# Causal attention scores on one Trainium2 core: half-empty diagonal blocks packed into a shared tile, stores in halves, and a new instruction order

## The chip, the core and the metric

The kernel runs on one core of one Trainium2 chip. The core has five engines with instruction streams of their own: PE (TensorE, matrix products into the PSUM memory), DVE (VectorE), ACT (ScalarE), POOL (GpSimd) and SP (SyncE, which here issues all DMAs). They meet only through semaphores. The metric is the time of one execution on the device in microseconds (us); lower is better. A time is given as the median of several runs.

## The reference

The input x has 2048 tokens of 512 channels in bfloat16. Two paths work on it, and a gate for each token mixes them:

```python
g = sigmoid((x * gate_w).sum(-1, keepdims=True))
a = A_ref(x, wq, wk, wv, wo, beta)      # attention with memory
b = B_ref(x, A_re, A_im, ..., Dskip)    # state-space convolution
return g * a + (1 - g) * b
```

Path A has 32 heads of width 16 and works through 4 segments of 512 tokens. Inside a segment it is causal softmax attention; across segments it reads a matrix memory M and a sum z, which are updated after each segment:

```python
for s in range(4):
    logits = einsum('bhqd,bhkd->bhqk', qs, ks) * scale + mask   # key > query is masked
    a_dot = softmax(logits) @ vs
    a_mem = (phi(qs) @ M) / (phi(qs) @ z + 1e-6)
    outs.append(g * a_mem + (1 - g) * a_dot)
    M, z = M + phi(ks).T @ vs, z + phi(ks).sum(tokens)
a = concat(outs) @ wo
```

Path B builds a convolution kernel of length 2048 for each of 512 channels from complex exponentials and convolves x with it by Fourier transforms.

## The kernel before

**Attention.** The function scores (lines 1021 to 1111) is called for each of 4 segments s and 4 groups hg of 8 heads, 16 groups in all. A group's even heads (gi = 0) and odd heads (gi = 1) lie in four strips of 32 partitions, r = 0 to 3, so that four matmuls, one in each strip, make the scores of four heads beside each other. For the odd heads, project (lines 992 to 1016) makes a second copy ko of the keys, in which the even heads' rows are zero (line 1004); mkT is that mask. Scores have keys on the partitions and queries along the free axis. The 512 keys of a segment are four blocks J of 128. Block J is needed by the queries from 128 J on, 512 - 128 J of them, and the first 128 of those form the diagonal block, which is masked.

For a group the scores fill five tiles of 128 partitions x 2048 columns (four heads x 512 columns, four PSUM banks), listed in kinds (lines 1027 and 1028): A0 has block 0 of the even heads, B0 blocks 1 and 3 of the even ones, C block 2 of both, A1 and B1 blocks 0, and 1 and 3, of the odd ones. For each tile the matmuls run (line 1073), then ACT takes the exponential of all 2048 columns into a buffer pT (line 1082). The diagonal is masked in one of two ways: in the first eight groups (pem, NPM = 8) a matmul of the identity with negm adds -30000 before the exponential (lines 1074 to 1081); in the last eight DVE multiplies the diagonal blocks of pT by mask01 (lines 1094 to 1096). The function pv (lines 1032 to 1048) then multiplies with the values: for each block J, each query block tb from J on and each head, one full matmul of 17 columns (16 values and a one, whose sum is the softmax denominator), 40 for one gi, 80 for a group. norm (lines 1050 to 1058) divides.

seg_tokens (line 931) makes the values vp of a segment; seg_state (line 950) updates the memory with buffers ek and rk; ophase (line 1113) reads it into o2 and transposes the sum.

**State-space path.** ssm_prep, ssm_powers and tables (line 1149) build the tables of exponentials, mostly on DVE in groups of two multiplications and an addition with a scratch tile t2. tail (line 1234) runs over 16 tiles t in each of two halves of the channels, named a and b: constants are loaded (CD, CT), x's transform is made and multiplied with the kernel's (line 1286), transformed back, and gathered in V2 with DMAs. At the end of tail, "fin", "fih" and "fir" are PE's operations of the output projection and the last transform; DVE first scales x (line 1332) and then mixes both paths into a tile ou (line 1337), and a DMA of 256 KB stores four token blocks (line 1340).

**What sets the order.** Every operation is recorded through op (line 161), or through dma and evac, which end there, with the tiles that it reads and writes. A string ORDER (lines 366 to 459) holds the order of all 1864 operations, made beforehand: each entry is the operation's number, an "a" or "v" where it is a copy that can run on ACT or on DVE (evac, lines 224 to 233; 166 entries have an a, 88 a v), and the buffers that it takes. replay (line 235) reads it, and emit (line 264) works out the waits and writes one instruction stream for each engine, in that order. Nothing is reordered when it runs. Because matmuls and copies are issued through helpers, the profile shows all matmuls but transposes at line 698, all DMAs at line 222 and the two kinds of copies at lines 226 (ACT) and 227 (DVE).

Scores always take PSUM banks 0 to 3 together (line 1062); pT has four buffers (NPT, line 354). Pools are laid out in lines 612 to 673.

Of the kernel before, what the change touches and what calls it, by code (L numbers as in the profile page):

```python
# [353 lines left out]
NPT = 4  # L354
# [12 lines left out]
21/0 192/0 193 194 195/0 394/0 196/0 10/4 197 208/1 9/3 0/0 26/3/1 15/0 27v 32/0 57/1 7/0 12/0 23/0 20/0 1237/0 16/0  # L367
11/1 17/0 58/0 14/2 13/5 33/0 41/1 42/2 36/3 37 34/9 60/1 35/12 38 39 40/6 1243/3/0 48/4 43/5 3/0 44 45 47/7 49/8
59v/0 46 51/6 50 1245/2 65v/4 53/13 52/10 64/0 591/0 66 1255/4/1 62/0 63 28/5/0 1253/6 54/9 55/0 56 1/0 1244a 76/4
74/1 75 77v/0 61a 203/7/1/2 86/3 89v/3 78 88/2 1254a 87 253/3/2/0 68/2 90 101v/1 70/1 100/3 98/0 99 69 82/6 29a 181/5  # L370
102 113v/2 110/3 80/1 1256a 112/0 81 206/0/0 111 204a 114 30/6/2 254a 1246a 31v 79 205 18/0 207a 184/3 124/7 1258/1
176/4 103 258/2/1/1 380/0 91 222/0/1 592/0 223 1257 122/0 123 593/0 259 134/2 125v/5 67 182/1 135/2 256/1/1 217/3/0/0
215/0 224 179/0 136 218 177/2 180/0 216a 94/3 146/0 115 1247 260 1000v/0 148/0 243/0/3 244 1271/0/1 147 257a 211/2 219
999v 161v/6 178 998v 126 127 162 185 802/0 245 997v 220 1001v/0 149v/7 1002 209/1 163 1272a 212a 231/0/0 232 158/0 233
1006/1 1005 1003/0 199/3 200 137v/8 1004 213/0 1009/0 214a 25 1007 160/5 1011 1259/2/0 210a 150 226/0/2 227 1260a
381/3 159 1269/0 1261/1 382 225/2 151 228 1270a 1008 138 255 1273 139 92/2 1262a 1263 238/3 239/0/1 240 1015/1 229
1010 1014 230 170v/9 1012/0 234 1016 1013 340/0/2 93 171 1023 241 1018/1 235/0 201/0 202/1 341a 236 383 104/3 1276/1/1
265/0/2 266 105/4 237/0 106 1017 172 267 1274/0 242 246 247 1238/2/0 1239a 1024/0 1277a 269/0/3 270 1275a 271 1019
248/1 261 116/3 1240/2 1278 1025 296/0/0/1 1020 297a 249 1250/1/1 1027/1 1241a 1242 274/0/0 275 268/0 272 276 1251a
386/2/1/2 387a 282/0/1 283 1026 284 250 1021/0 117/2 1028 273 277 1029 299/3/0 1248/1 1022 278/2 1036/1 279 385/0 118  # L380
1266/2/0 1300/0 300a 1249a 1267a 286/0/2 287 337/2/2/0 5/0 24 221/3/0 1264/1 280/1 1035 298 1032 1037 130/7 1252 288
1279/1 310/0/3 311 1265a 301/0/0/0 128/0 262 312 281/1 285 289 290 306/0/2 302 307 1038 338a 1039/0 308 1033/1 1040
291/3 1030/0 292 263/0 446/2/1 293 303 342/1/1/1 1031 1295/3/1 323/0/1 304 1297/0 324 343 344 1268 1296a 447a 1298a
1303/1/0 1034 1301/3 1302v 129 325 401/2 1044/0/0 402v 1045 1047/3 1048 183 450/0 142/5 140/2 141 388 345 315/0/0
154/0 1304a 316 339 1050/2 1051 1052v 1041/1 1042 1061v/0 1057v/0 1059v 1063/1 1065 1049a 1060v 1058v 251/3 1046a
309/2 317 107a/4 327/0/2 328 252a/0 1066/0 294/0 313 1299 314 318 803/3 1043a 1062 1067 1064 319/2 389/1/0 1054/0 329
1075/0 1068 320 108 1071 1072/1 152/3 119a/1 390a 1074 321/0 349/0/3 350 1076 804 1285/1/1 83v/0 1084/0 1083 1073
399/2 351 322/3 84 295a 353/0/0 1077 1286a 1305 1085 95v/2 1086 354 1053 326 1287/0 395/1 330 1288v 400a 331 332/3 355
153 1087/1 396a 71a/6 358/0/1 359 305/0 346 1313/2/0 360 1311/1 4/0 85 333 1312a 1055 1289 1088 72 1314a 1078/1 347
334 1095 1096/0 366/0/2 367 1290/1/1 368 109 352/2 1292/0 1293a 1291a 6/0 1056 1315 2/0 1079 73 1097 1080 1294 120 121  # L390
22 493/3/0/1 370/0/3 371 494a 1081/1 1280/0/0 356 357 361 397/1 495 1089 143v/5 1090/0 1282/3 372 1281a 408/0/0 1082
409 1318/0/1 1091 1098 1069/1 362/4 1283a 1284 1070 363 144 1099/0 410 164/1 805 1319a 398a 365/3 412/0/1 413 335/0
369 373 374 364/1 375/5 96 1308/1/0 414 336a 165/6 376 1093/1 1306/2 1309a 425/0/2 426 1092 1307a 1100 97 411/0 1316/1
415 427 1310 1094 1317a 377 166 443/2/2/0 131v/8 132 429/0/0 430 1320 1328/0 1110/1/0 1111 444a 1107/3 1112v 1108
1101/2 167a/3 173v/9 168 1102 1104/1 1105 431 155a/7 198 1118v/0 156 1120v 169 1117a 1123/1 157 1121v/0 417/0/3 174
1330/0 1125 1119v 418 1126/0 445 1122 1127 1131 1132/0 1133 1124 393/1 1106a 416 496/1/2 1382/1 419 497a 1103a 1109a
1128 475/0/1 476 477 1356/2 133 420 1329/0 1116 1113 424/1 391/1 428 1331/2/0 1135/0 421/0 1355/1 1134 1129/1 175 1114
1115 422 451/3/0/0 432 433 434/1 392 1332a 1334 1343/0 1333 458/0/3 459 460 1130 544/2/0 452 423/0 1341/1 1136 1144/1
1143 435 264 462/0/2 594 545a 463 464 1335/0/1 403/2/1/1 145 1342/0 384/0 1145 467/0/0 348 468 436 1336a 461/1 378/0
404 465 1138/0 1147/1 1146 1337/1 453 466 454 405 1137 1139 1148 1141/0 1338/3/0 1156/1 1140 1344/2/1 469 1354/0 1345a  # L400
1339a 479/0/3 480 474/2 1347 1348/3/0 470 379a 481 471/1 1349a 478 523/0/2 1357/0/2 448/0 1346 1368/0 1340/0 524 1358a
1155 1359 472 482 1360 449 406 483 484/3 1361/3/1 407/0/1 1350/0 473/1 1351/1/1 1157 485 1158 1159/1 1367/1 525 1369/0
486 1362a 1381/1 515/0/3 1142 516 437/1/2/0 455 1352a 1353 438 1408/2 1374/1/0 517 456 501/6/1/1 1363/1 1364/7/0 498/1
502 439 440 1160 608/0/1 1365a 1380/0 1370/2/0 503 527/0/0 528 1149 1375a 522/3 8/0 1371a 1150/0 609a 1387/1/1
541/2/1/0 529 526 1383/0/1 654/5/2/2 542a 549/2/0/0 1152 1395/0 1384a 1388a 441/0 1151 1372 1153/1 530 1373 1376/0
1394/0 1154 500/1 600/4/1 550 1377/1/1 655a 487/3/4/1 442a/0 1434/1 1385 1386 1366 1378a 531 499 551 532/5 1167/5/0
1164/0 1161/1 1162 601a 552 602/0 1393/1 1165 488 1166a 533 1407/1 489 1170/2 1168 1169a 1171 1179a/0 1172a 1389/0
1390/0/0 1163a 490 504 1391a 1181v/0 506/0/1 507 1396/2/2 1178v 1186/0 1185 186/1 543 1180v 1177a 1400/0/0 1397a 1187
1182 187/0 1406/0 1379 612/2 1409/1/0 508 1183/1 1192/0 190/0 510/0/0 1401a 1410a 1184 1191 1188 1193 1398 1399 1173
1195/1 595 1194 534/0 1198/0 511 1447/0 1413/0/1 1392 505/1 553 512 1196 613a 1412 1402/1 1189/1 1403/3/1 556/0/2 557  # L410
1203 554 1411 1197 509/2 513 514 518 1190 1414a 535/0/3/0 1415/0 1404a 558 1416/3/0 560/0/3 561 1433/1 519/0 1417a
1199 520 536 1432/1 1460/2 521 1446/0 1445/0 1200 537 1435/3/1 1439/2/0 1405 1204/0 1436a 538 1201/1 1499/1 657/3/2
1437 1321/0 1205 559/0 562 1202 1209 1448/1/2 1438 573/0/1 574 1418 1459/1 658a 1452/3/1 1449a 1440a 1441/1 1451 563
597/2/0/1 575 564 1450 565/0/0 566 1210/0 546/1 598a 1453a 1442/1/1 491/2 1206 1454/0 1211 1207/1 1443a 1472/0 1176
# [114 lines left out]
def build_graph(nc, es, A_x, A_wq, A_wk, A_wv, A_wo, A_beta, B_A_re, B_A_im, B_B_re, B_B_im,  # L529
# [911 lines left out]
```

## Time and profile before

| what | value |
|---|---|
| time, median of 3 runs | 303.54 us (302.54 to 307.06) |
| profiled execution | 304.81 us; its span 303.0 us |
| mean granted TensorE clock in it | 0.963 |
| ACT exponentials of scores, line 1082 | 80, 152.0 us |
| ACT copies, line 226 | 158, 88.9 us busy |
| DVE copies, line 227 | 53 from PSUM in float32, 34.9 us busy |
| DVE masks, line 1094 | 40, 22.5 us busy |
| PE matmuls, line 698 | 3767, 254.7 us busy |
| DMA | 47.85 MB, mean 158 GB/s |

The profile shows one execution. Busy times are unions, so an instruction that overlaps the one before it on its engine adds less to them than its own duration. A line of a group reads: line, engine, operation, destination and source with their partitions x elements, how many; then busy us and mean ns of one; then the idle time of the engine just before them and what ended it. The chain of work follows the last instruction back to what released it at each step. A matmul's end is modelled and includes the draining of the array, so its duration (some 0.17 us for 17 columns) is much longer than the step from one to the next.

### The profile page before, as it was taken

Reading aid. Unit: us, or ns where it says so; the run is one execution under the profiler, and the core shown is the slowest. Engines: PE = TensorE matmul, PEld = TensorE weight load, DVE = VectorE, ACT = ScalarE, POOL = GpSimd, SP = SyncE. Lnnn points to the kernel's source line nnn. Section 1 sums busy time; section 2 is a strip of 40 time slices with the busy share of each in tenths; the row PEclk is TensorE's granted clock in tenths of the full one; section 3 lists DMA queues with packets and bytes.
Section 4 is the critical chain, followed back from the end, with each engine's and each line's share of the span. In section 5 each row is a group of like instructions: output and inputs, shape, how many; then the busy total and the mean of one; then the engine's idle time right before and its main releaser. Section 6 shows DMA issues by size and latency. Waiting matters only on the chain.

```text
span 303.0 us, 9317 instructions
## 1 busy us (share of the span) xinstructions
PE 260.7 (86%) x3855; PEld 176.8 (58%) x3855; DVE 280.6 (93%) x694; ACT 258.4 (85%) x309; POOL 3.3 (1%) x10
## 2 busy tenths in 40 slices
PE   1569799898879867999999999999999998899990
PEld 1334444555544645766766576766677656679870
DVE  3999989999999898999999989998999999998992
ACT  2799999999999998999899999999999899983000
POOL 2000000000000000000000000000000000000000
PEclk9997978999996999999999999999999999999996
DMA  5998422612231464665666667687756677731333
GB/s 140 269 209 190 95 90 71 177 68 60 63 121 50 120 177 122 180 173 149 191 210 164 206 181 236 206 244 216 211 176 208 200 233 235 217 104 27 105 110 111
DMA packets 55546, 47.85 MB, mean 158 GB/s; under 512 B 22736, under 2 KB 50384, under 8 KB 55504
## 3 DMA queue, kind: packets, MB, share of 16 engines
q1 hardware_dynamic: 55504, 47.26, 54.5%
q8 instruction: 30, 0.49, 0.7%
q14 instruction: 12, 0.10, 0.1%
HBM read 29.02 MB, written 6.29 MB: 117 GB/s over the span
## 4 chain that ended last, share of the span: by engine, by line
PE 31%; DVE 27%; ACT 26%; DMA 5%; issue 5%; SPq 4%; DVEq 0%; ACTq 0%
PE psum L698 30%; ACT sb L1082 11%; ACT sb L226 10%; DMA sb<-sb 4%; SPq L222 4%; DVE sb L1337 4%; DVE sb L227 4%; DVE sb L1332 3%; DVE sb L1286 3%; DVE sb L1094 3%; ACT sb L808 3%; DVE sb L1177 2%; DVE sb L1184 2%; DVE sb L1180 2%; DMA sb<-in_B_log_dt_dram 1%
## 5 line engine op out<-in xcount | busy, mean ns | idle before, releaser
L698 PE MATMUL psum<-sb 128*128 128x17 bf16 (+11 forms) x3767 | 254.7, 233 | 24.0 <-ACT sb L1082 11.7
L698 PEld LDWEIGHTS psum<-sb 128*128 128x128 bf16 (+3 forms) x3767 | 169.9, 99 | 104.3 <-ACT sb L1082 27.3
L1082 ACT ACTIVATE sb<-psum 128x2048 bf16<-128x2048 f32 x80 | 152.0, 1900 | 3.4 <-PE psum L698 2.2
L226 ACT ACTIVATE sb<-psum 128x512 bf16<-128x512 f32 (+2 forms) x158 | 88.9, 618 | 8.6 <-PE psum L698 8.1
L227 DVE CAST sb<-psum 128x512 bf16<-128x512 f32 (+1 forms) x53 | 34.9, 671 | 2.4 <-PE psum L698 2.3
L1177 DVE TENSOR_TENSOR sb<-sb 128x512 bf16<-128x512 bf16 (+3 forms) x52 | 34.2, 659 | 0.0
L1180 DVE TENSOR_TENSOR sb<-sb 128x512 bf16<-128x512 bf16 (+3 forms) x52 | 33.7, 654 | 0.1
L1184 DVE TENSOR_TENSOR sb<-sb 128x512 bf16<-128x512 bf16 (+3 forms) x52 | 33.6, 660 | 0.1
L1286 DVE TENSOR_TENSOR sb<-sb 128x1024 bf16<-128x1024 bf16 x32 | 21.4, 678 | 2.2 <-issue 1.3
L1094 DVE TENSOR_TENSOR sb<-sb 128x1024 bf16<-128x1024 bf16 (+1 forms) x40 | 22.5, 573 | 0.4 <-ACT sb L1082 0.4
L1332 DVE SCALAR_TENSOR_TENSOR sb<-sb 128x256 f32<-128x256 bf16 x32 | 14.3, 475 | 0.0
L1337 DVE SCALAR_TENSOR_TENSOR sb<-psum,sb 128x256 bf16<-128x256 f32 x32 | 13.1, 477 | 1.0 <-PE psum L698 1.0
L1057 DVE TENSOR_TENSOR sb<-psum,sb 128x256 bf16<-128x256 f32 x32 | 13.4, 418 | 0.2
L808 ACT ACTIVATE sb<-sb 128x512 f32<-128x512 f32 x18 | 11.5, 654 | 0.0
L1054 DVE RECIPROCAL sb<-psum 128x16 f32<-128x16 f32 x32 | 8.0, 249 | 0.6 <-PE psum L698 0.6
L1134 DVE TENSOR_TENSOR sb<-psum,sb 128x512 bf16<-128x512 f32 x12 | 8.2, 687 | 0.3
L809 DVE TENSOR_TENSOR sb<-sb 128x256 f32<-128x256 f32 x18 | 7.3, 414 | 0.9 <-ACT sb L808 0.9
L1013 ACT ACTIVATE sb<-sb 128x512 bf16<-128x512 bf16 x12 | 7.6, 637 | 0.0
L810 DVE SCALAR_TENSOR_TENSOR sb<-sb 128x256 f32<-128x256 f32 x18 | 7.4, 417 | 0.0
L962 ACT ACTIVATE sb<-psum 128x512 bf16<-128x512 bf16 x12 | 7.4, 614 | 0.0
L756 PE MATMUL psum<-sb 128*128 128x128 bf16 x24 | 2.7, 279 | 5.0 <-DMA sb<-c_ident 4.6
L959 PE MATMUL psum<-sb 128*128 128x128 bf16 x48 | 4.9, 227 | 2.2 <-ACT sb L226 2.2
(67 smaller groups left out, 102.1 us busy)
## 6 DMA issues: line engine op xcount, KB each, us to landing
sb<-c_DNM SPq DMA_DIRECT2D x32, 320.0 KB, 3.5
sb<-c_DNM SPq DMA_DIRECT2D x32, 192.0 KB, 3.0
sb<-sb SPq DMA_DIRECT2D x84, 64.0 KB, 2.9
sb<-in_A_x_dram SPq DMA_DIRECT2D x9, 512.0 KB, 4.9
scr_Z<-sb SPq DMA_DIRECT2D x16, 256.0 KB, 2.3
sb<-scr_Z SPq DMA_DIRECT2D x32, 128.0 KB, 3.1
sb<-sb SPq DMA_DIRECT2D x32, 128.0 KB
out_dram<-sb SPq DMA_DIRECT2D x8, 256.0 KB, 2.2
```

Of the source, the lines that this page charges most:

```text
L226: fa = lambda e: e.activation(dst(), src(), ACT.Copy)
L227: fd = lambda e: e.tensor_copy(dst(), src())
L698: mm = lambda e, o_, l, r_, st, sp, **kw: e.matmul(o_, lhsT=l, rhs=r_, start=st, stop=sp, skip_group_check=True, **kw)
L808: op("ACT", ("As", 512), lambda e, sq=sq, Z=Z: e.activation(ap(sq, n=512), ap(Z, n=512), ACT.Square), r=[Z], w=[sq], key=PW[h] + PWS * k)
L1082: o = op("ACT", ("Ax", 2048), lambda e, P=P, pT=pT: e.activation(ap(pT, n=2048), ap(P, n=2048), ACT.Exp, scale=0.25), r=[P], w=[pT])
L1094: op("DVE", ("V2", 128 * nb), lambda e, pT=pT, dims=dims: e.tensor_tensor(ap(pT, dims=dims + [[1, 128]]), ap(pT, dims=dims + [[1, 128]]), ...
L1177: op("DVE", ("V2" if n > 1 else "V1", 256 * n), lambda e: e.tensor_tensor(run(tile, ne, dst, 1), run(tile, ne, src, sstep), ap(pw, cl * 51 ...
L1180: op("DVE", ("V2" if n > 1 else "V1", 256 * n), lambda e: e.tensor_tensor(run(t2, n, 0, 1), run(tile, ne, src, sstep), ap(pw, cl * 512 + 2 ...
L1184: op("DVE", ("V2" if n > 1 else "V1", 256 * n), lambda e: e.tensor_tensor(D_(), D_(), ap(t2, n * 128, [[-n * 128, 2], [2 * n, 64], [1, 2 * ...
L1286: op("DVE", ("V2", 1024), lambda e, Y=Y, XAB=XAB, K3=K3: e.tensor_tensor(ap(Y, dims=[[512, 2], [1, 512]]), ap(XAB, dims=[[512, 2], [1, 512 ...
L1332: op("DVE", ("V1", 256), lambda e, xd=xd, b4=b4: e.scalar_tensor_tensor(ap(xd, n=256), ap(xns[b4 // 4], (b4 % 4) * 512 + half * 256, n=256 ...
L1337: op("DVE", ("V1", 256), lambda e, ou=ou, b2=b2, j=j, b4=b4, P=P, xd=xds[j]: e.scalar_tensor_tensor(ap(ou, (2 * b2 + j) * 256, n=256), ap( ...
```

## The change

**Scores.** The queries of a diagonal block's first half need only the block's first 64 keys. These parts, for all four blocks, for even and odd heads and for two neighbouring groups hg and hg + 1, go into one "low" tile: the even heads' 64 keys on partitions 0 to 63, the odd heads' 64 keys on partitions 64 to 127, 64 queries for each block, 4 blocks x 2 groups x 64 = 512 columns for each of 4 strips. The other tiles begin at each block's query 64: A has blocks 0 and 3 (448 + 64 columns), B blocks 1 and 2 (320 + 192). So two groups have nine tiles of 2048 columns, where they had ten, and the tile C is made in even groups only. ko is laid out anew (192 columns for each block: 64 of the even rows, then 128 of the odd), by two DVE instructions, of 512 and 256 elements, in place of one. Both groups of a pair are projected together.

**Masks.** In A and B a mask now covers 64 columns at two places, 128 columns for each strip. The low tile is masked on DVE, 2048 elements in one instruction, in all 16 groups (DQL = 1); its matmul mask is left out.

**Values.** pv leaves out the diagonal block: 24 full matmuls for one gi. A new function pvd makes the diagonal at the end of each gi, with pairs of matmuls on half of the array's columns each: 64 queries from the low tile with vL, 64 from pT with vp, 32 of them for one gi. vL is a copy of the values in which the odd heads' values of each block's first 64 keys stand on partitions 64 to 127: two DMAs of 136 KB for each segment, and one clearing by POOL at the start. The values are now stored with even heads first, then odd.

**Stores and buffers.** Each output store of 256 KB becomes two of 128 KB, each as soon as its half is made. Buffers: pT 4 to 3, plus one for the low tile; ek, o2 and t2 2 to 1; CT of half b 5 to 4; vL has one.

**Order.** ORDER is another one, with 1873 entries; 186 have an a, 68 a v. It is left out below.

```diff
-NPT = 4
+NPT = 3
+NPL = 1
+DQL = 1
...
-        op("DVE", ("V4", 512), lambda e: e.tensor_scalar(ap(ko, n=512), ap(kT, n=512), ap(mkT, n=1), None, ALU.mult), r=[kT, mkT], w=[ko])
+        op("DVE", ("V4", 512), lambda e: e.tensor_scalar(ap(ko, 64, [[192, 4], [1, 128]]), ap(kT, dims=[[128, 4], [1, 128]]), ap(mkT, n=1), None, ALU.mult), r=[kT, mkT], pw=[ko])
+        op("DVE", ("V4", 256), lambda e: e.tensor_scalar(ap(ko, dims=[[192, 4], [1, 64]]), ap(kT, dims=[[128, 4], [1, 64]]), ap(mkT, 1, n=1), None, ALU.mult), r=[kT, mkT], pw=[ko])
...
+        for gi in range(2):
+            S.dma(lambda gi=gi: ap(vL, 272 * gi, [[544, 4], [1, 272]], p0=64 * gi, np_=64), lambda gi=gi: ap(vp, 272 * gi, [[544, 4], [1, 272]], np_=64),
+                  139264, r=vparts + [vp] + ([vL] if s == 0 else []), pw=[vL])
...
-                for tb in range(J, 4):
+                for tb in range(J + 1, 4):
...
+        def pvd(gi):
+            T = PV[gi]
+            src = [q[1:] for q in diag if q[0] == gi]
+
+            def f(e):
+                for J, pT, off in src:
+                    for r in range(4):
+                        o = (4 * hg + r) * 17 + J * 544 + gi * 272
+                        mm(e, ap(T, J * 68 + r * 17, n=17, np_=64), ap(low[0], r * 512 + (hg % 2) * 256 + J * 64, n=64), ap(vL, o, n=17), False, True, tile_position=(0, 0))
+                        i = mm(e, ap(T, J * 68 + r * 17, n=17, p0=64, np_=64), ap(pT, r * 512 + off, n=64), ap(vp, o, n=17), False, True, tile_position=(0, 64))
+                return i
...
+            ent = [] if isl else [(1, 0), (2, 320)] if nm[0] == "B" else [(0, 0), (3, 448)]
...
+                if isl:
+                    for h_, (q_, _, k_, _, _) in enumerate(two):
+                        for J in range(4):
+                            for r in range(4):
+                                i = mm(e, ap(P, r * 512 + 256 * h_ + 64 * J, n=64), ap(k_, 192 * J, n=128, p0=32 * r, np_=32),
+                                       ap(q_, 128 * J, n=64, p0=32 * r, np_=32), h_ == 0 and J == 0, not pem or bool(DQL), tile_position=(32 * r, 0))
+                    return i
...
-            S.dma(lambda g4=g4: bass.AP(out, g4 * 2048 + half * 256, [[8192, 128], [512, 4], [1, 256]]),
-                  lambda ou=ou: ap(ou, dims=[[256, 4], [1, 256]]), 262144, r=[ou])
+                S.dma(lambda g4=g4, b2=b2: bass.AP(out, g4 * 2048 + b2 * 1024 + half * 256, [[8192, 128], [512, 2], [1, 256]]),
+                      lambda ou=ou, b2=b2: ap(ou, b2 * 512, [[256, 2], [1, 256]]), 131072, r=[oup[b2]])
...
-            project(s, hg)
+            if hg % 2 == 0:
+                S.key = TA0 + GA * (i0 - 4)
+                project(s, hg)
+                project(s, hg + 1)
```

316 lines of the change are left out of this document (166 added, 150 removed).

## The prediction

> **What bounds the kernel now.** I read the page first: the busy shares, the forty slices, and the chain that ended last.
>
> ```profile
> span 303.0 us, 9317 instructions
> ...
> PE 260.7 (86%) x3855; PEld 176.8 (58%) x3855; DVE 280.6 (93%) x694; ACT 258.4 (85%) x309; POOL 3.3 (1%) x10
> ...
> PE   1569799898879867999999999999999998899990
> ...
> DVE  3999989999999898999999989998999999998992
> ACT  2799999999999998999899999999999899983000
> ...
> PEclk9997978999996999999999999999999999999996
> ...
> PE 31%; DVE 27%; ACT 26%; DMA 5%; issue 5%; SPq 4%; DVEq 0%; ACTq 0%
> ```
>
> Three engines are full at once. DVE leads with 280.6 us. The chain is shared almost equally (31, 27 and 26%), so it hops between engines that are full, and a saving on one engine alone is paid out only where the chain lies on it. The windows view splits the span into the stretch in which the attention exponentials set the pace, the stretch in which both halves of the state-space path run beside them, and the end.
>
> ```profile
> core 0: us, PE busy (x) PEld busy (x) DVE busy (x) ACT busy (x) POOL busy (x), PEclk, DMA share, GB/s
> 6.00:128.00 122.00, 98.66 (x1444) 58.23 (x1445) 116.76 (x305) 116.75 (x153) 0.65 (x1) 0.93 0.49 130
> 128.00:236.00 108.00, 104.93 (x1653) 74.27 (x1652) 103.68 (x242) 103.43 (x122) 0.66 (x1) 1.00 0.67 199
> 236.00:297.00 61.00, 56.05 (x755) 43.53 (x752) 58.77 (x144) 36.67 (x33) 0.00 (x0) 1.00 0.51 153
> ```
>
> The reader should see that PE has room only in the first stretch (98.66 of 122). In the second all three are at 96 to 97%. In the third DVE leads (58.77 of 61), PE follows, and ACT has nothing to do near the end.
>
> **The change on ACT and DVE.** The durations are in the groups by shape, and in the chain, which shows what each instruction adds when it follows another.
>
> ```profile
> L1082 ACT ACTIVATE sb<-psum 128x2048 bf16<-128x2048 f32 x80 | 152.0, 1900 | 3.4 <-PE psum L698 2.2
> L227 DVE CAST sb<-psum 128x512 bf16<-128x512 f32 x50 | 33.5, 682 | 1.5 <-PE psum L698 1.3
> L1094 DVE TENSOR_TENSOR sb<-sb 128x1024 bf16<-128x1024 bf16 x24 | 16.3, 679 | 0.4 <-ACT sb L1082 0.4
> L1177 DVE TENSOR_TENSOR sb<-sb 128x2048 bf16<-128x2048 bf16 x12 | 14.6, 1215 | 0.0
> L1094 DVE TENSOR_TENSOR sb<-sb 128x512 bf16<-128x512 bf16 x16 | 6.6, 414 | 0.0
> L817 DVE CAST sb<-sb 128x512 bf16<-128x512 f32 x15 | 6.2, 419 | 0.0
> L1004 DVE TENSOR_SCALAR sb<-sb 128x512 bf16<-128x512 bf16 x16 | 5.5, 347 | 0.4 <-ACT sb L226 0.4
> L818 DVE TENSOR_SCALAR sb<-sb 128x256 bf16<-128x256 bf16 x20 | 4.4, 227 | 0.0
> ```
>
> ```profile
> 20.22 2.43 ACT sb L226 x5
> 161.62 1.14 DVE sb L1177
> 185.34 1.78 ACT sb L1082
> 189.61 1.20 DVE sb L227 x2
> 295.40 1.57 DVE sb L1337 x4
> ```
>
> A DVE evacuation of 512 columns lasts 0.68 but adds 0.60 (1.20 for two), so about 0.08 of each DVE instruction lies under its neighbour. An ACT evacuation adds 0.49 (2.43 for five), an exponential 1.78.
>
> Exponentials: 16 groups with 5 tiles are 80; afterwards 16 with 4 and one tile for each of 8 pairs are 72. ACT loses 8 x 1.78 = 14.2 us.
>
> Evacuations moved: in the order's list the entries marked for ACT go from 166 to 186, those marked for DVE from 88 to 68. Twenty move. Laid against the order in which the code makes the operations, 13 of them net are PSUM evacuations of 512 columns; the other seven are four casts of powers (the row of L817), one table copy, one lag-table evacuation and one transposed input, on average 0.4 for DVE and 0.5 for ACT. DVE loses 13 x 0.60 + 7 x 0.4 = 10.6; ACT gains 13 x 0.49 + 7 x 0.5 = 9.9. ACT net: -4.3.
>
> Masks on DVE: before, the last eight groups have 16 of 512 and 24 of 1024 elements, 16 x 0.414 + 24 x 0.679 = 22.9. Afterwards they have 32 of 512, and every pair, those of the first eight groups too, has one of 2048: 32 x 0.414 + 8 x 1.215 = 23.0. The sum is the same, but 4 x 1.14 = 4.6 us of it come into the first groups, which had none on DVE.
>
> The second masked copy of the keys: 16 of 256 elements, 0.227 - 0.08 = 0.15 each, 2.4 us (between 16 x 0.08 and 16 x 0.35, the row of L1004; nearest is L818, the same form and size). DVE net: -10.6 + 0.1 + 2.4 = -8.1 us.
>
> **The change on PE.** Short windows, each cut around one operation, price it; x also counts up to five matmuls of the neighbours that reach in. In order: one scoring tile of 4 matmuls of 512 columns, 32 or 16 rows each, which run beside each other; 16 full matmuls of 17 columns; 4 full ones of 512; 64 of 40 columns on half the array's columns each; a scoring tile of two widths; 4 mask matmuls of 2 x 128; 8 of 128.
>
> ```profile
> 187.17:187.50 0.33, 0.33 (x4) 0.10 (x5) 0.33 (x1) 0.33 (x1) 0.00 (x0) 1.00 0.59 157
> 187.50:187.91 0.41, 0.41 (x20) 0.41 (x17) 0.41 (x2) 0.40 (x2) 0.00 (x0) 1.00 0.10 25
> 188.34:189.21 0.86, 0.86 (x6) 0.39 (x4) 0.86 (x2) 0.86 (x1) 0.00 (x0) 1.00 0.79 279
> 170.68:171.81 1.12, 1.12 (x68) 1.09 (x65) 1.12 (x3) 1.06 (x2) 0.00 (x0) 1.00 0.60 170
> 184.43:184.76 0.33, 0.33 (x9) 0.12 (x9) 0.33 (x2) 0.33 (x2) 0.00 (x0) 1.00 1.00 374
> 162.43:162.87 0.44, 0.44 (x6) 0.38 (x4) 0.44 (x2) 0.44 (x2) 0.00 (x0) 1.00 1.21 233
> 162.87:163.31 0.44, 0.44 (x10) 0.44 (x8) 0.44 (x2) 0.44 (x2) 0.00 (x0) 1.00 0.81 313
> ```
>
> So a full matmul of 17 columns adds 0.0256 us, a half one 0.0175. A change between full array and row strips costs about 0.11 (0.33 for the strips against 0.86 / 4 = 0.22 for the same 512 columns).
>
> Values: a group's 80 full matmuls become 48 full and 64 halves, which come in two blocks of 32. Removed 32 x 0.0256 = 0.82; added 64 x 0.0175 = 1.12, and two entries into the half arrangement at 0.1. That is +0.5 for a group, +8 for 16. Lower end: a pair of halves for one full, and no change of arrangement that was not there, 0. Upper end: every half as a full one, +1.02 for a group, +16. I take +8, from the row that has halves.
>
> Scores: tiles of 448 + 64 and 320 + 192 columns cost 0.33, as both rows of scoring tiles show, whatever the widths. Two C tiles (0.66) become one low tile of 32 small matmuls: at least 0.33 (512 columns again), at most 32 x 0.0256 + 0.11 = 0.93. I take the middle, 0.6: 8 x (0.6 - 0.66) = -0.5 (-2.6 to +2.2).
>
> Masks by matmul, first eight groups only: 2 tiles of 4 x 0.055 and 3 of 4 x 0.11 (1.76) become 4 tiles of 4 x 0.055 (0.88); the low tile has none. -7.0.
>
> PE net: +8 - 0.5 - 7.0 = +0.5 us; but -3.2 for the first eight groups, where PE has room, and +3.8 for the last eight, where it has hardly any.
>
> The Trainium skill, TensorEngine Tiling (Array Packing), Performance Considerations, says that each matmul carries about 60 cycles of overhead, and that one with free dimension 1 takes as long as one with 60. TensorE: Matmul & The Clock Gate, Back-to-back issue gap, gives that floor as about 25 ns. Full matmuls here agree (0.0256); the halves do not (0.0175). By the rule the values would cost PE +16 in place of +8.
>
> **DMA, POOL, buffers.**
>
> ```profile
> sb<-sb SPq DMA_DIRECT2D x84, 64.0 KB, 2.9
> out_dram<-sb SPq DMA_DIRECT2D x8, 256.0 KB, 2.2
> ```
>
> Two copies of 136 KB for each segment shift the values' first 64 keys for the odd heads. The nearest row, copies of 64 KB inside the buffer memory, lands after 2.9; I take 3 for these. The copies' tile has one buffer, so a segment's copies wait for the last value matmuls of the segment before, and behind them on SP stand the loads of the tail's constants. In the new order 4 to 6 us of DVE work (by the durations above) lie between each second copy and its first reader: covered, and 4 x 3 = 12 us if that cover is gone. POOL clears that tile once, beside 300 us of idle POOL: nothing. The stores: the last one starts with its last half only. Between the last DVE instruction (295.40 + 1.57 = 297.0) and the end lie 6.0 us, of which landing is 2.2; half the bytes give at most 1.1, I take -0.4. Its eight more issues lie between DVE instructions of the end: nothing.
>
> Buffers go from two to one for ek, o2 and t2, from five to four for CT of the second half, from four to three plus one for the exponentials. ek and o2 are needed once in a group, t2's readers and writers are all on DVE in order with a multiplication between: nothing, and at most 52 x 0.08 = 4 us for t2. The exponentials' buffers are the rival below: a buffer is now held until the diagonal's value matmuls.
>
> **The sum.** DVE -8.1, ACT -4.3, PE +0.5. By the chain's shares of 303 us: DVE 82 us x 8.1 / 280.6 = -2.4, ACT 79 x 4.3 / 258.4 = -1.3, PE 94 x 0.5 / 260.7 = +0.2, end of store -0.4: -3.9. The profiled execution took 304.81 (span 303.0 and 1.8 around it) and would become 300.9. The median of the three runs is 1.3 below it, and the prediction is a median: 303.5 - 3.9 = 299.6.
>
> **The rivals.**
>
> *DVE is the one bound.* It is busy 279.2 of the 291 us before 297, and the end is its own. Then all of -8.1 and the store's -0.4 come out: 295.0. Against it: PE's 97% in the second stretch.
>
> *PE takes over.* From 128 on, PE has 3.1 + 5.0 us idle, and the last eight groups give it 3.8 more. If it is the bound there, DVE's saving is lost and the time is 303.5 + 3.8 - 0.4 = 306.9. Against it: PE's busy time contains the draining of matmuls, so there is more room than it shows.
>
> *A half matmul costs as much as a full one.* A mechanism of the value blocks alone: +7.6 for the last eight groups in place of +3.8, with PE the bound: 303.5 + 7.6 - 0.4 = 310.7. That is the rule of the Trainium skill above, taken for halves. The 64 halves in 1.12 us speak against it.
>
> *The low tile's chain holds PE.* This is the one on the slower side. PE works in order.
>
> ```profile
> PEld psum L698 <- ACT sb L1082: 27.3, 50, 1.5
> PE psum L698 <- ACT sb L1082: 11.7, 23, 1.4
> PEld psum L698 <- DVE sb L1094: 1.7, 6, 0.6
> ```
>
> PE waits for exponentials already, but hardly for masks. Now the diagonal's value matmuls need the low tile's exponential (1.78), its mask on the fullest engine (1.14) and their own 0.56: 3.5 us from scores to the release of two buffers, of which the fourth exponential needs one. Behind them on PE stand the next scores, and ACT waits for those. Uncovered in all 8 pairs it is 28 us, and 36% of that takes 299.6 past +2%; with half of it the time is 313.6. Against it: the new order puts 8 to 25 other PE operations between a low tile's scores and its first reader.
>
> **How the numbers follow.** A measurement of this kernel tells about 2% (6.1 us) from no change. My forecast, the shared chain, 299.6 with its own range 296.5 to 303: 0.38. DVE alone, 295.0: 0.29. PE takes over, 306.9: 0.15. Halves as full, 310.7: 0.04. The low tile's chain, 313.6: 0.14. Faster by over 2% is below 297.4: the DVE case and a small part of the first, 0.32. Slower by over 2% is above 309.6: the last two, 0.18. Within 2%: 0.50. The range leaves out those last two, 0.18: from 293.2 (DVE alone, with the store's 1.1 and the key copies at 0.08: 295.0 - 0.7 - 1.1) to 308.2 (PE's takeover with the last four low tiles at 0.93: 306.9 + 4 x 0.33).
>
> **What would show it.** ACT: 72 exponentials, about 254 us busy. DVE about 272. PE about 261, with a block of 32 half matmuls in 0.56 and the low tile in 0.33 to 0.93. If PE waits for the mask of 2048 elements, the low tile's chain is right; if PE is above 98% from 128 us on while DVE falls below 92%, PE took over. The prediction is wrong in its core if DVE's busy time falls by 8 and the span by 8 too, or if no engine's sum moves as stated.

## The result, and the profile after

The changed kernel takes 302.62 us (median of 20 runs, 299.32 to 307.61), the kernel before, on the same chip, 304.38 us (20 runs). The ratio is 0.990, with an interval from 0.987 to 0.993. A second measurement of the same kernel, called again below, gave 303.06 against 304.53 us, ratio 0.994 (0.991 to 0.997). The change saves 1.8 to 3.0 us by these two ratios, about 0.6 to 1.0%. The first ratio leaves out the six slowest of the changed kernel's 20 executions and none of the other kernel's; the medians of all of them differ by 1.8 us, a ratio of 0.994 like again's. All lines of the changed kernel are from again, whose profiled execution took 303.31 us; its mean granted clock was 0.936, the median of again's runs is 0.952.

The page of the changed kernel, with the rows that answer to those of before: span, busy time, slices, granted clock, chain.

```profile
span 301.5 us, 10764 instructions
...
PE 257.8 (86%) x4554; PEld 184.1 (61%) x4591; DVE 272.6 (90%) x690; ACT 253.4 (84%) x321; POOL 5.2 (2%) x11
...
PE   2668598978788799889999899989999999999990
...
DVE  1999999889999999899999998699888998887992
ACT  2899999999999999989999999888998999982100
...
PEclk9999576699789879999999999999999999999997
...
ACT 33%; PE 32%; DVE 26%; issue 3%; DMA 3%; SPq 1%; DVEq 0%
```

DVE's busy time fell by 8.0 (280.6 to 272.6), ACT's by 5.0 (258.4 to 253.4), PE's by 2.9 (260.7 to 257.8). The span fell by 1.5. So most of it became idle time: DVE's idle time in the span grew from 22.4 to 28.9, ACT's from 44.6 to 48.1. The same stretches as before, the last one cut at 299 in place of 297:

```profile
core 0: us, PE busy (x) PEld busy (x) DVE busy (x) ACT busy (x) POOL busy (x), PEclk, DMA share, GB/s
6.00:128.00 122.00, 98.90 (x1690) 61.14 (x1706) 117.78 (x310) 116.60 (x163) 0.66 (x1) 0.86 0.52 138
128.00:236.00 108.00, 102.14 (x1940) 76.04 (x1963) 100.59 (x243) 98.66 (x121) 0.66 (x1) 1.00 0.67 195
236.00:299.00 63.00, 55.85 (x921) 46.16 (x914) 54.19 (x139) 36.08 (x37) 0.00 (x0) 0.99 0.55 164
```

In the second stretch all three engines have room now (102, 101 and 99 of 108; they had 105, 104 and 103). No engine is full, and yet the kernel is hardly faster. What fills the room stands in the view of waits, first of the changed kernel, then of the one before, over the whole span:

```profile
ACT sb L226 <- PE psum L705: 15.1, 22, 4.2
PE psum L705 <- ACT sb L1133: 9.4, 14, 2.1
...
DVE sb L227 <- PE psum L705: 4.9, 7, 1.6
ACT sb L1133 <- PE psum L705: 4.7, 12, 0.6
...
DVE sb L1376 <- DMA sb<-in_A_x_dram: 1.7, 1, 1.7
...
PEld psum L705 <- DVE sb L1141: 0.2, 1, 0.2
```

```profile
ACT sb L226 <- PE psum L698: 8.1, 15, 2.2
DVE sb L227 <- PE psum L698: 2.3, 6, 1.0
ACT sb L1082 <- PE psum L698: 2.2, 7, 0.5
```

ACT waits for PE 19.8 us where it waited 10.3, DVE's evacuations (its copies out of PSUM) 4.9 where they waited 2.3. PE in its turn waits 9.4 for exponentials (11.7 before). New is the wait of DVE for a load of x. Part of ACT's wait lies in the last stretch, where ACT has nothing to do anyway; in the second stretch alone (128 to 236 us) the copies of both engines wait longer for PE too, first the changed kernel, then the one before:

```profile
ACT sb L226 <- PE psum L705: 5.7, 13, 1.2
DVE sb L227 <- PE psum L705: 4.9, 7, 1.6
```

```profile
ACT sb L226 <- PE psum L698: 2.5, 8, 0.5
...
DVE sb L227 <- PE psum L698: 1.0, 4, 0.4
```

### The profile page after: what moved, and what is told of

The parts are those of the page before. It is cut to its first block, busy times and chain, and to the rows that moved or that the text cites. A ratio compares the mean times of both kernels' runs of the same rounds, so it can differ in the third digit from the quotient of the medians.

```text
span 305.8 us, 10764 instructions
## 1 busy us (share of the span) xinstructions
PE 256.7 (84%) x4554; PEld 184.5 (60%) x4591; DVE 272.6 (89%) x690; ACT 253.2 (83%) x321; POOL 5.2 (2%) x11
## 4 chain that ended last, share of the span: by engine, by line
ACT 38%; PE 34%; DVE 16%; DMA 5%; issue 3%; SPq 1%; DVEq 0%; ACTq 0%
PE psum L705 34%; ACT sb L1133 19%; ACT sb L226 13%; DMA sb<-sb 4%; ACT sb L815 3%; DVE sb L1227 2%; DVE sb L1381 2%; DVE sb L1329 2%; DVE sb L227 2%; DVE sb L1223 1%; ACT sb L976 1%; DVE sb L1220 1%; ACT sb L823 1%; SPq L222 1%; DMA sb<-c_ident 1%
## 5 line engine op out<-in xcount | busy, mean ns | idle before, releaser
L705 PE MATMUL psum<-sb 128*64 128x17 bf16 (+11 forms) x4466 | 250.2, 222 | 33.1 <-ACT sb L1133 10.7
L705 PEld LDWEIGHTS psum<-sb 128*128 128x128 bf16 (+3 forms) x4503 | 177.9, 104 | 103.4 <-issue 24.2
L1133 ACT ACTIVATE sb<-psum 128x2048 bf16<-128x2048 f32 x72 | 137.6, 1911 | 7.6 <-PE psum L705 7.0
L226 ACT ACTIVATE sb<-psum 128x512 bf16<-128x512 f32 (+2 forms) x173 | 99.4, 636 | 17.6 <-PE psum L705 17.1
L227 DVE CAST sb<-psum 128x512 bf16<-128x512 f32 (+1 forms) x39 | 26.1, 673 | 6.3 <-PE psum L705 6.0
L1141 DVE TENSOR_TENSOR sb<-sb 128x512 bf16<-128x512 bf16 (+1 forms) x40 | 22.6, 570 | 1.9 <-ACT sb L1133 1.9
L763 PE MATMUL psum<-sb 128*128 128x128 bf16 x24 | 3.1, 310 | 6.0 <-DMA sb<-c_ident 5.1
L227 DVE COPY sb<-psum 128x1024 bf16<-128x1024 bf16 x2 | 2.6, 1280 | 6.2 <-PE psum L763 6.2
```

What stands on the lines that cost most here:

```text
L226: fa = lambda e: e.activation(dst(), src(), ACT.Copy)
L227: fd = lambda e: e.tensor_copy(dst(), src())
L705: mm = lambda e, o_, l, r_, st, sp, **kw: e.matmul(o_, lhsT=l, rhs=r_, start=st, stop=sp, skip_group_check=True, **kw)
L1133: o = op("ACT", ("Ax", 4 * W), lambda e, P=P, pT=pT, W=W: e.activation(ap(pT, n=4 * W), ap(P, dims=[[512, 4], [1, W]]), ACT.Exp, scale=0.2 ...
L1141: op("DVE", ("V2", 2048 if isl else 512), lambda e, pT=pT, md=md, m0=m0: e.tensor_tensor(ap(pT, dims=md + [[1, 64]]), ap(pT, dims=md + [[1 ...
```

## The experiments

Ratios are to the kernel before, measured beside each kernel, with their intervals. The theory behind the prediction was that the chain is shared and a saving is paid by the chain's shares. The rivals were one engine as the bound. A number of us got from two ratios carries their intervals, some 1.3 us either way.

**The same kernel again, and one engine relieved at a time.** The reliefs leave work out. For PE, pvd's second half of blocks:

```diff
                 for J, pT, off in src:
+                    if J > 1:
+                        continue
```

For DVE, the masks' width; for ACT, the exponentials' columns from the fifth group on:

```diff
-                    ap(pT, dims=md + [[1, 64]]), ap(pT, dims=md + [[1, 64]]), ap(mask01, m0, [[0, k_[1]] for k_ in md] + [[1, 64]]), ALU.mult),
+                    ap(pT, dims=md + [[1, 16]]), ap(pT, dims=md + [[1, 16]]), ap(mask01, m0, [[0, k_[1]] for k_ in md] + [[1, 16]]), ALU.mult),
...
-            o = op("ACT", ("Ax", 4 * W), lambda e, P=P, pT=pT, W=W: e.activation(ap(pT, n=4 * W), ap(P, dims=[[512, 4], [1, W]]), ACT.Exp, scale=0.25), r=[P], w=[pT])
+            o = op("ACT", ("Ax", 4 * W), lambda e, P=P, pT=pT, W=W: e.activation(ap(pT, dims=[[512, 4], [1, 448 if 4 * s + hg > 3 else 512]]), ap(P, dims=[[512, 4], [1, 448 if 4 * s + hg > 3 else 512]]), ACT.Exp, scale=0.25), r=[P], w=[pT])
```

> The changed kernel once more, timed beside the others. Shared chain (my forecast's theory: three engines take turns, PE is short of room from 128 us on): 0.985 to 0.993 of before, and in an undisturbed profile DVE's idle time grows by what its busy time fell, while ACT and DVE wait longer for PE than before (before: ACT copies for PE 8.1 us, exponentials for PE 2.2 us). Low tile's chain: PE waits for DVE's masks of 2048 elements, over 3 us in all (before 2.1 us for all masks).

> The changed kernel with the diagonal's value matmuls of blocks 2 and 3 left out (16 of 32 halves in each block, so the output is not the reference's): PE loses 512 x 0.0175 = 9.0 us, half of it in the last eight groups, nothing else changes. Shared chain: a third to a half of it, 3 to 4.5 us under the changed kernel. PE alone the bound from 128 us on: 4.5 us, and the same order would give nothing for DVE. Another engine the bound: under 1 us.

> The changed kernel with each mask multiplication cut to 16 of 64 columns (part of the masked scores stays in, the output is not the reference's): DVE loses 32 x 0.16 + 8 x 0.8 = 11.5 us by the durations of 512, 128 and 2048 elements. Shared chain: DVE has room now, 1 to 3 us under the changed kernel. DVE still the bound: 8 us or more. Low tile's chain: 0.8 us for each of 8 low tiles, about 6 us, with the waits of PE for masks gone.

> The changed kernel with 448 of each 512 columns in the exponentials of the last 12 groups (the other columns keep old values, the output is not the reference's): ACT loses 54 x 0.21 = 11.5 us. Shared chain: a third, 3 to 5 us under the changed kernel. PE alone the bound: under 1.5 us. ACT alone: 9 us or more.

| kernel | busy time taken away | median | ratio |
|---|---|---|---|
| again | | 303.06 | 0.994 (0.991 to 0.997) |
| PE less | PE 257.8 to 248.6 | 302.74 | 0.995 (0.991 to 0.998) |
| DVE less | DVE 272.6 to 261.9 | 302.06 | 0.994 (0.991 to 0.998) |
| ACT less | ACT 253.4 to 242.7 | 302.01 | 0.989 (0.985 to 0.994) |

Nine to eleven us less on one engine move the median by 0.3 to 1.1 us. By the ratios PE's and DVE's reliefs give nothing that can be told (0.995 and 0.994 against 0.994), ACT's 1.4 us with an interval that reaches zero. None of the three is the bound by itself. PE's takeover is out: with PE relieved 4.5 us should have followed. DVE alone is out as well. The shared chain was missed too: it had named 3 to 4.5 us for PE, 1 to 3 for DVE and 3 to 5 for ACT, and for again 0.985 to 0.993.

**All three at once.** The three edits together.

> The three reliefs together (PE -9.0, DVE -11, ACT -11 us by their own runs, which each moved the time by under 1.5 us; parts of the value products, masks and exponentials are left out, the output is not the reference's). Shared chain: what no single engine gives back all three give together, 6 to 10 us under the changed kernel. Fixed delays (DMA, semaphores, clock) as the bound: under 3 us.

Measured: 299.94 us, ratio 0.983 (0.979 to 0.987). The page of that kernel:

```profile
span 297.0 us, 9742 instructions
...
PE 245.1 (83%) x4044; PEld 172.6 (58%) x4079; DVE 261.1 (88%) x690; ACT 242.3 (82%) x321; POOL 5.2 (2%) x11
...
ACT 31%; PE 27%; DVE 24%; DMA 7%; issue 5%; SPq 4%; DVEq 0%; ACTq 0%
```

Each engine has 11 to 13 us less to do, the ratio is 0.011 lower than again's 0.994: 3.3 us (some 1.8 to 4.9). Even a relief of all three is paid to some 30% only, below the 6 to 10 us of the shared chain. That the rest stays as waits of one engine for another, in an order that is fixed, is a reading and not shown: the under 3 us that the expectation gave to fixed delays (DMA, semaphores, clock) lies within the interval as well.

**The same reliefs in the kernel before.** DVE's masks cut to 48 of 128 columns of a block, ACT's exponentials as above; both leave that work out.

```diff
-                ap(pT, dims=dims + [[1, 128]]), ap(pT, dims=dims + [[1, 128]]),
-                ap(mask01, dims=[[0, k_[1]] for k_ in dims] + [[1, 128]]), ALU.mult), r=[mask01], w=[pT])
+                ap(pT, dims=dims + [[1, 48]]), ap(pT, dims=dims + [[1, 48]]),
+                ap(mask01, dims=[[0, k_[1]] for k_ in dims] + [[1, 48]]), ALU.mult), r=[mask01], w=[pT])
```

> The kernel before, with VectorE's 40 masks cut to 48 of 128 columns of each block, so that part of the masking is left out and VectorE has some 10.7 us less to do (280.6 to 270), as much as the cut took from it in the changed kernel, where it moved the time by nothing that could be told. By the shares of the chain that the prediction went by: 82 x 10.7 / 280.6 = -3.1 us, ratio 0.990. If VectorE was the bound before and no longer is: -8 to -10, ratio 0.97. If no engine's relief alone is paid out, before as after: 0 to -1.5, ratio 0.995 to 1.

> The kernel before, with the 60 exponentials of the groups from the fifth on cut to 448 of 512 columns of each block, so that an eighth of their columns is left out and ScalarE has some 60 x 0.2 = 12 us less to do (258.4 to 246.5). By the shares of the chain: 79 x 12 / 258.4 = -3.7 us, ratio 0.988. If ScalarE's relief alone is not paid out: 0 to -1.5, ratio 0.995 to 1.

DVE went from 280.6 to 271.7, the median from 304.84 to 304.53, ratio 0.997 (0.994 to 1.001): by the ratio -0.9 us. ACT went from 258.4 to 246.8, the median to 303.51, ratio 0.994 (0.991 to 0.997): by the ratio -1.8 us. So one us of DVE was worth 0.10 us in the kernel before (0 to 0.22 by the interval), one of ACT 0.16 (0.07 to 0.25). The chain's shares had said 82 / 280.6 = 0.29 and 79 / 258.4 = 0.31, above both intervals. The page with DVE relieved:

```profile
PE 254.4 (84%) x3825; PEld 176.5 (58%) x3855; DVE 271.7 (90%) x694; ACT 258.0 (85%) x309; POOL 3.3 (1%) x10
...
ACT 39%; PE 29%; DMA 10%; DVE 10%; issue 5%; SPq 4%; DVEq 0%; ACTq 0%
```

DVE's share fell from 27 to 10%, ACT's rose from 26 to 39%. That looks as if the chain had left DVE for an engine that was nearly as late, but the shares move as much where DVE keeps its work. DVE is busy 272.6 us in again, with 26% of the chain. Two kernels that are described below have it at 272.6 (the masks issued twice) and 272.5 (the load of x moved), with 13 and 15%:

```profile
ACT 40%; PE 33%; DVE 13%; DMA 6%; issue 4%; SPq 2%; DVEq 0%; ACTq 0%
```

```profile
ACT 41%; PE 30%; DVE 15%; DMA 6%; issue 4%; SPq 1%; DVEq 0%; ACTq 0%
```

So a share from one profile is no price.

**The other direction: 20 evacuations given back to DVE.** The change moved 20 copies from DVE to ACT. Here 20 evacuations of 512 columns, spread over the new order, go back: their entries in ORDER get a v for an a, as 219 does in the line shown. They aren't the same 20, since the order is another one.

```diff
-1001v/0 221a 208a 223a 146/3 201/0 1000v 1008 148/1 803/0 1258 196/0 215 219a 236/0/0 237 238 147 1012 160/2 1013/0
+1001v/0 221a 208a 223a 146/3 201/0 1000v 1008 148/1 803/0 1258 196/0 215 219v 236/0/0 237 238 147 1012 160/2 1013/0
...
```

> The changed kernel with 20 PSUM evacuations of 512 columns, spread evenly over the order, given back from ScalarE to VectorE; nothing else is changed. VectorE's busy time rises by 20 x 0.67 = 13 us to about 286, ScalarE's falls by 20 x 0.6 = 12 to about 241. Shared chain, by the changed kernel's shares (ScalarE 33, VectorE 26%) and the added time of one instruction (0.60, 0.49): +3.5 - 3.8 = about 0, ratio to the kernel before 0.993. VectorE is the bound: +12 us, ratio 1.03. Work added to a full engine costs more than work taken away brings back, since the other engines' order is fixed: +2 to +5 us, ratio 1.00 to 1.01.

Measured: 311.49 us, ratio 1.021 (1.016 to 1.026), 2.7% above again's 0.994, or 8.2 us.

```profile
span 308.7 us, 10773 instructions
...
PE 257.6 (83%) x4554; PEld 183.2 (59%) x4591; DVE 283.2 (92%) x710; ACT 246.1 (80%) x301; POOL 5.2 (2%) x11
...
DVE 58%; PE 24%; DMA 6%; issue 6%; ACT 2%; SPq 2%; DVEq 0%; ACTq 0%
```

DVE got 10.6 us more, ACT 7.3 less, and DVE now has 58% of the chain. Work taken from DVE was worth a tenth of itself, work added to it costs three quarters. The expectation "more than work taken away brings back" had the direction, and 2 to 5 us was too little. With this number of copies back on DVE the changed kernel is 2% slower than the one before, at a DVE time only 2.6 us above it (283.2 against 280.6). What stays open is how much of this is DVE's load, and how much is that these entries stand where the order wanted ACT.

**TensorE's clock.** Again's page shows PEclk at 5 to 8 tenths in eight slices of the first 120 us (5, 7, 6, 6, then 7, 8, 8, 7), where the kernel before has four (7, 7, 8, 6). The change took mask matmuls out of just these groups. The theory: less matmul work lowers the clock, and the slower PE eats the saving. Two kernels put work back, one the masks of the first eight groups (each twice), one the 32 matmuls of the x transform (each twice).

```diff
-                    for r in range(4):
+                    for r in (0, 1, 2, 3) * 2:
...
-                    op("PE", c_pe("F", 512), lambda e, P=P, xj=xj, bl=bl, hf=hf: mm(e, ap(P, n=512), ap(W1T, hf * 128, n=128), ap(xj, bl * 512, n=512), True, True),
+                    op("PE", c_pe("F", 512), lambda e, P=P, xj=xj, bl=bl, hf=hf: [mm(e, ap(P, n=512), ap(W1T, hf * 128, n=128), ap(xj, bl * 512, n=512), True, True) for _ in range(2)][1],
```

> The changed kernel with each mask matmul of the first eight groups issued twice (the masked scores get -60000 in place of -30000, the result is the same): PE gets 128 matmuls of 128 columns more, +7 us at full clock, the amount that the change took from there. Clock theory (in the first 128 us PE's clock is halved for 3.4 us or more after each stretch of 3.4 us with little matmul work; the change took work out of there, and the half-clock time rose from 17 to 34 us): mean granted clock from 0.95 to 0.965 or more, half-clock time 20 us or less, and 1.5 to 3 us faster than the changed kernel although PE does more. Engine-sum theory: 0 to +4 us, slower.

> The changed kernel with each of the 32 matmuls of x's first transform issued twice (the second overwrites the first, the result is the same): +6.9 us of PE at full clock, as many columns as in the run with the masks twice, but in other places and ahead of copies that ACT waits for. Clock theory: clock up to 0.96 or more and 0.5 to 2.5 us faster than the changed kernel. Engine-sum theory: 0 to +4 us.

Masks twice: 306.75 us, 1.004 (1.001 to 1.008), mean clock 0.962 (median of its runs). Transform twice: 304.15 us, 0.995 (0.992 to 0.998), clock 0.980. Again has 0.952, the kernel before 0.97. The slices of the second kernel:

```profile
PEclk9999599999999979999999999999999999999997
```

So the clock rose with the added work, and the time did not follow the clock. With the masks twice the ratio is 0.010 above again's, 3.1 us slower at a higher clock. With the transform twice the clock is above that of before, and the ratio is again's. There a gain by the clock could be hidden by the cost of the added matmuls (32 of 0.22 us, 7 us); the run does not separate the two, but the intervals leave no more than about 1 us of a net gain where the theory named 0.5 to 2.5. As an explanation of the missing saving the clock is not supported.

**The low tile's mask moved to PE** in the first eight groups (DQL = 0; in the order the four masks stand on PE right behind their tile's scores):

```diff
-DQL = 1
+DQL = 0
```

> The changed kernel with the low tiles of the first eight groups masked by matmuls too (DQL = 0), as the other tiles there: four DVE multiplications of 2048 elements go (-4.6 us of DVE), sixteen matmuls of 512 columns come (+3.4 us of PE), in the stretch where PE has room. Clock theory: half the added columns of the other two runs, clock 0.955 to 0.965, 1 to 2 us faster than the changed kernel. DVE the bound: 4 us faster. Low tile's chain: 1 us for each of the four, 4 us faster. PE the bound: 2 to 3 us slower.

Measured: 305.91 us, 1.003 (1.000 to 1.006), with DVE at 268.8: 0.9% or 2.6 us above again, though the fullest engine had 3.8 us less. Every theory that named a gain missed; the loss is the one named for PE as the bound (2 to 3 us), although PE's relief gave nothing. As with the masks twice, work added to PE in the first groups costs, and work taken from it brings nothing back. In this order the low tile's mask is better left on DVE there.

**The late load of x.** The new wait at the end was traced to the change of buffers. The third quarter of x (xn2, 512 KB) takes the place of 4 KB of attention buffers in each partition, formerly exactly ek and rk with two buffers each, whose last use is early. With one buffer for ek these 4 KB reach into qT, which the last group's scores read. In the order the load went from the 1353rd place of 1864 to the 1740th of 1873. Here xn2 lies over the transposed x and is issued as soon as the last projection has read that:

```diff
-    xnPs = [mkpool("xn%d" % i, 4096, 1, 2) for i in range(3)]
+    xnPs = [mkpool("xn%d" % i, 4096, 1, 2) for i in range(2)]
+    a = XT0
+    xnPs.append(mkpool("xn2", 4096, 1, 2))
...
+        if g4 == 2:
+            o.deps += [d for t in xTT for d in t.rd]
```

> The changed kernel with one load moved. With one ek buffer in place of two, the 4 KB for the third quarter of x (512 KB in all), which the end adds to the output, reach over the first query buffer, so the load waits for the last group's scores: it is issued at 269.9 us, and VectorE waits 1.68 us for it until 275.34 and then runs without idle time to the end. Here it lies over the buffer of transposed x and is issued some 25 us earlier; nothing else is changed. If this wait is where part of the saving went, the wait is gone and the time falls by up to 1.7 us (ratio to the kernel before about 0.988 where the changed kernel has 0.993). If TensorE, which is full from 268 to 276, sets that stretch, VectorE waits for TensorE in its place and the time stays (0.993).

Measured: 304.79 us, 1.000 (0.997 to 1.003): slower than again, if anything. The timeline of DVE, first of again, then of this kernel (start, duration; in brackets the idle time before it and its cause), and then of this kernel's SP:

```profile
275.34 1.67 DVE L1376 SCALAR_TENSOR_TENSOR sb<-sb 128x256 f32<-128x256 bf16 x4 [1.68 <-DMA sb<-in_A_x_dram]
```

```profile
249.79 1.29 DVE L1331 TENSOR_TENSOR sb<-sb 128x1024 bf16<-128x1024 bf16 x2 [2.12 <-DMA sb<-sb]
```

```profile
243.27 0.33 SPq L222 DMA_DIRECT2D sb<-in_A_x_dram  x1
243.65 3.10 SPq L222 DMA_DIRECT2D sb<-sb  x5
```

The wait at the end is gone, and another of 2.12 us has come: five copies are issued on SP right behind the load, and DVE's next multiplication reads one. From 248 to 252 all three engines stall: PE is busy 2.61 us of the 4.00, DVE 2.21 and ACT 2.81, where again has 3.94, 3.12 and 4.00. That the load ahead of them held these copies up is read from one profile and not tested by itself.

The chain of work says more about the end: first again's, then this kernel's with the row of DVE that follows it (start, duration):

```profile
264.94 10.79 PE psum L705 x188
```

```profile
267.08 16.46 PE psum L707 x240
```

```profile
283.57 0.88 DVE L1383 SCALAR_TENSOR_TENSOR sb<-psum,sb 128x256 bf16<-128x256 f32 x2 [1.11 <-PE psum L707]
```

In again the chain lies on PE until 275.73, through the whole of DVE's wait for the load (until 275.34). Without that wait it lies on PE still longer, and DVE waits 1.11 us for PE. So the expectation's first reading, that the wait was where part of the saving went, is not borne out. The second, that PE sets this stretch, agrees with both chains; what it did not foresee is the new wait for copies. Why the ratio is 0.006 above again's is not settled by this.

## Why the prediction was right, and where it was not

Within 2% was forecast as the likeliest, and it is so. The 302.62 us lie near the end of the forecast's own range (296.5 to 303; again's 303.06 is just past it) and 3.0 us above its 299.6. Of these, 0.8 is the kernel before, which took 304.38 beside it and not 303.5. As a saving, 3.9 us were forecast, and the medians give 1.8. The rows that price the steps, by shape, of again:

```profile
L1133 ACT ACTIVATE sb<-psum 128x2048 bf16<-128x2048 f32 x72 | 137.4, 1909 | 5.2 <-PE psum L705 4.7
...
L227 DVE CAST sb<-psum 128x512 bf16<-128x512 f32 x37 | 25.2, 683 | 4.8 <-PE psum L705 4.5
...
L1141 DVE TENSOR_TENSOR sb<-sb 128x512 bf16<-128x512 bf16 x32 | 12.9, 411 | 2.0 <-ACT sb L1133 1.9
...
L1141 DVE TENSOR_TENSOR sb<-sb 128x2048 bf16<-128x2048 bf16 x8 | 9.7, 1210 | 0.2 <-ACT sb L1133 0.2
...
L824 DVE CAST sb<-sb 128x512 bf16<-128x512 f32 x11 | 4.4, 419 | 0.0
L1019 DVE TENSOR_SCALAR sb<-sb 128x256 bf16<-128x256 bf16 x16 | 4.3, 266 | 0.0
```

- *DVE, -8.1:* measured -8.0. The 13 evacuations went (50 to 37, 33.5 to 25.2 us), four casts of powers too (15 to 11), the masks cost 12.9 + 9.7 = 22.6 for the 23.0 expected. The second key copy lasts 0.266, a little over the row taken for it (0.227).
- *ACT, -4.3:* measured -5.0. The 8 exponentials took 14.6 (152.0 to 137.4) for 14.2.
- *PE, +0.5:* measured -2.9, though PE's busy time is a rough scale here: it contains the half-speed stretches, and differs by 3 us between two profiles with the same PE program (257.8 here, 254.5 with the load of x moved). The short windows of again say more: the low tile, a scoring tile of two widths, and a block of 32 halves.

```profile
168.03:168.37 0.34, 0.34 (x33) 0.29 (x33) 0.34 (x3) 0.24 (x1) 0.00 (x0) 1.00 1.05 407
170.55:170.88 0.33, 0.33 (x9) 0.12 (x9) 0.33 (x1) 0.33 (x2) 0.00 (x0) 1.00 0.70 177
179.07:179.68 0.61, 0.61 (x36) 0.59 (x33) 0.61 (x2) 0.61 (x2) 0.00 (x0) 1.00 0.85 336
```

The low tile's 32 matmuls take 0.34 in this window, the lower bound, not the 0.6 between the bounds: 8 x (0.34 - 0.66) = -2.6 in place of -0.5. A block of 32 halves takes 0.61 with its change of arrangement, where 0.56 + 0.1 was taken: 2 x 0.61 - 0.82 = +0.4 for a group, +6.4 in place of +8. With the masks' -7.0 that is -3.2. So four strips run beside each other for small matmuls as for large ones, and halves do not cost as much as full ones: (0.61 - 0.1) / 32 = 0.016 us each, where a full one takes 0.0256. The rule of the Trainium skill (TensorEngine Tiling (Array Packing), Performance Considerations), taken for halves, is not borne out here. (The time of that rival doubled all of the +3.8; only the values' +4 doubles, to 1.02 x 8 = 8.2, with the scores' -0.25 to 7.9, which gives 311.0 in place of 310.7. Nothing hangs on it.)
- *The store, -0.4:* 0. The last DVE instruction ends at 295.5, the span at 301.5:

```profile
294.34 1.18 DVE sb L1381 x3
```

That leaves 6.0 us, as before; 128 KB land in 1.9 us where 256 KB took 2.2.
- *Buffers, nothing:* ek's second buffer hid the load of x. This step overlooked that the end's buffers lie over those of attention. The new wait is 1.7 us in the profile, but again's chain lies on PE through it, and the time gave nothing back when it went, as above. What the other buffers cost was not tried.
- *The sum by the chain's shares, -2.4 and -1.3:* this is the step that was off. With the rates that the reliefs gave in the kernel before, 0.10 x 8.0 + 0.16 x 5.0 = 1.6 us; the upper ends of the rates give 3.0, and the forecast's shares gave 3.7. That 1.6 comes so close to the measured 1.8 is partly luck: the sum leaves out PE's -3.2 and whatever the new order and the fewer buffers cost, which no run separates. A reading that fits, and is not shown step by step: the chain goes through one engine at each moment, but another is only a little less late, so that 8 us taken from one of three engines that wait for each other buy the small distance to the next, again and again.
- *Rivals:* DVE as the one bound fell in the core test that the prediction named: DVE fell by 8, the span by 1.5. PE's takeover is contradicted by PE's relief, and its sign did not come: from 128 us on PE is busy 158.0 of 171 us, 92% and not 98. PE does hold a piece of the end, by the chain from 264.94 to 275.73. The low tile's chain was hidden: PE's weight loads wait for a mask once, 0.2 us, and the row of the 2048 masks has 0.2 us of idle time before it.

## What to carry to other kernels

Where three engines are each 84 to 93% busy in one fixed order, read the chain's shares as a list of who can be late, not as prices: relieve one engine on the chip (cut a width, skip a block) and see what one us of it is worth, in both directions. Here one us less on DVE was worth 0.1 in the kernel before and nothing that can be told in the changed one; one us more, moved there from ACT, cost about 0.8. A wait that a view lists is worth removing only where the chain passes it: look which engine the chain lies on at that time. When a buffer is taken away, follow what lies over its memory later, and when a DMA is moved, name what is queued behind it.

## What the runs showed of the hardware

The granted TensorE clock goes to half for whole stretches of 3.41 us, in again for 34 us altogether, in the profile of before for 17. None of the falls follows an idle stretch: in the 3.41 us before each, PE was busy 1.50 to 2.10 us in again, 1.59 to 2.75 in before. The windows of again, cut at those edges:

```profile
13.81:17.22 3.41, 1.17 (x3) 0.15 (x1) 3.41 (x10) 3.41 (x7) 0.00 (x0) 1.00 1.33 295
...
27.46:30.87 3.41, 1.50 (x15) 0.54 (x14) 3.41 (x15) 3.41 (x8) 0.00 (x0) 1.00 0.58 152
30.87:34.28 3.41, 1.79 (x50) 1.16 (x51) 3.41 (x14) 3.41 (x5) 0.00 (x0) 0.50 0.99 227
34.28:37.70 3.42, 2.57 (x31) 1.27 (x31) 3.42 (x11) 3.42 (x6) 0.00 (x0) 0.50 0.42 90
37.70:41.11 3.41, 3.37 (x33) 1.46 (x32) 3.41 (x7) 3.24 (x5) 0.00 (x0) 0.50 0.34 101
41.11:44.52 3.41, 3.25 (x66) 1.89 (x64) 3.41 (x11) 3.41 (x5) 0.00 (x0) 1.00 0.39 115
...
51.34:54.75 3.41, 3.41 (x70) 2.25 (x70) 2.62 (x9) 3.15 (x4) 0.00 (x0) 0.50 0.24 84
```

PE was busy 1.50 of 3.41 us when the clock fell first, and the clock came back after a stretch with 3.37. PE's busy time alone does not decide: the stretch from 13.81 with 1.17 was followed by full clock (17.22 to 20.63 has 1.00), the one from 51.34 with 3.41 by another at half (54.75 to 58.17 has 0.50). The Trainium skill, TensorE: Matmul & The Clock Gate, Part 1 (the clock gate), gives windows of about 3.4 us and half rate after an idle one. The length agrees; here a window that was busy to 44% was enough. What decides was not settled.
